# Local attention and an MLP: transposing one head's two parts at a time, and value products on four corners of the array

## The chip, the cores and the metric

The kernel runs on one core of one Trainium2 chip. The time is device microseconds of one execution; the runs shown are compared by their median. Engines are named as in the profile: PE is TensorE's matmul side and PEld its weight loads, DVE is VectorE, ACT is ScalarE, POOL is GpSimd, SP is SyncE, which issues nearly all DMA here.

## What is computed

Local attention for 8 batches and 8 heads over 576 positions of 64 channels, then an MLP over the 4,608 tokens. Every query sees at most 32 keys: heads 0 to 3 the last 32 positions, heads 4 to 7 every fourth of the last 128.

```python
scores = scale * np.matmul(q, k.transpose(0, 1, 3, 2))
scores = np.where(masks[None, :, :, :], scores, -1000000000.0)
scores = scores - np.max(scores, axis=-1, keepdims=True)
attn = np.exp(scores)
attn = attn / (np.sum(attn, axis=-1, keepdims=True) + 1e-09)
out = np.matmul(attn, v)            # [8, 8, 576, 64]
x = out.transpose(0, 2, 1, 3).reshape(4608, 512)
h = x @ w_in                        # w_in 512 x 2048
sp = np.maximum(h, 0.0) + np.log1p(np.exp(-np.abs(h)))
y = (h * erf(sp)) @ w_out           # w_out 2048 x 512
```

## The kernel before, in words

**Units.** A pair of heads of one batch is an item (32 items, heads h = 0 and 1). Its 576 queries are cut in strips of 32; a strip looks at 64 keys. Eight strips are a unit, 72 units in all, and a unit has two parts p = 0, 1 of four strips each.

**One unit's attention.** `scores` (L200): 16 products, a strip and head each, on eight places of PE's array (head h on rows 64h to 64h+63, strip r on columns 32r to 32r+31); head 0's results end in the PSUM bank sp0, head 1's in sp1. The first 256 columns of these banks hold two units' scores in turn. `mask_max` (L211) on DVE adds the mask and takes row maxima, four instructions (part outside, head inside). `exponents` (L221) on ACT, `normalize` on DVE (L232, L233) and POOL (L234). `transposes` (L239): two 128x128 transposes, one per part, each with both heads' 64 keys, into `turn_place`; `turned` (L243) copies the 256 columns to pT in SBUF. `values` (L257): 16 products, strip and head, with 64 keys contracted, 64 channels and 32 queries. Head h's keys lie on partitions 64h and up, its channels on 64h and up, so the products use two corners of the array, (0, 0) and (64, 64). All results of a unit go to `place`: 256 columns of one bank. `rows_hi` (L298) on ACT copies them, rounded, into rows of x, and `rows_lo` (L303) on DVE subtracts to get the rest; both go by the pieces that `pieces` cuts, at item borders and, for the dilated heads, every 144 positions.

**Banks.** The eight PSUM banks are sp0, sp1, tx, h and acc0 to acc3. Units below FREE = 15 use acc banks, (u+1) % 4, for `place` and `turn_place`, since the MLP does not use them yet. Later units use tx for `place` (its second half for the second unit of a pair) and columns 256 to 511 of sp0, or sp1 for the second of a pair, for `turn_place`. The framework that writes the semaphores keeps the order of the program between instructions of two engines on one bank whenever either order could clash, two readers included.

**The order of work** is written out by hand. First 14 first visits (`first_visit`), with visit n doing the scores of unit n and the value products of unit n - 3; weights are read and split meanwhile (`prep_act`, `prep_dve`). Then a loop over half steps x of the MLP: `mm1` (L478) fills bank h, `take` (L486) copies it out on DVE, `mm2` (L519) adds the gated result of two steps before into acc. The table made by `visits` says at which half steps units are attended: one unit each at x = 0 to 6 and at three more, then 25 pairs at 2 to 5 half steps' distance, then the last unit alone. In such a half step `turn` stands ahead of mm2, and `attend` behind it: value products of the ready units, scores of the next ones, row copies; then the maxima.

```python
    def attend(ready, scored):
        for u in ready:
            values(u)
        for u in scored:
            scores(u)
        for u in ready:
            rows_hi(u)
```

## Time and profile before

| | |
|---|---|
| median of 3 runs | 956.28 us (956.1 to 956.96) |
| profiled execution | 957.19 us, span 955.4 us |
| granted clock of the core | 0.998 |
| PE, PEld busy | 931.9 us, 768.3 us |
| ACT, DVE, POOL busy | 633.6, 559.1, 74.3 us |
| HBM read, written | 74.15 MB, 27.26 MB |

A row of a group reads: line, engine, operation, out<-in by the program's names, partitions x elements, count, then busy time, mean of one in ns, and the idle time ahead with what ended it. A row of the order of time reads: start, length, engine, line, the same names, count, and in brackets the idle time ahead. In the table of stretches each engine has its busy time and, in brackets, its number of instructions; behind them the granted clock, the DMA share and GB/s. A product in FP32 stands as two matmul records and two weight loads.

### The profile page before, as it was taken

The page shows a single profiled execution, that of the slowest core. Times are in us where ns is not written, and L with a number is a line of the kernel's source. Part 1 is how long each engine was busy: PE and PEld are TensorE (multiplying, and loading weights), DVE is VectorE, ACT ScalarE, POOL GpSimd, SP SyncE. Part 2 cuts the span into 40 slices and gives each one's busy share as a digit, 9 for nine tenths or more (in the row PEclk, how much of TensorE's full clock was granted, in tenths as well). Part 3 has the DMA queues.
Part 4 walks back from the last instruction along what each step waited for, and adds up shares of the span by engine and source line. Part 5 has one row for each costly group of instructions (what it writes and reads, how often), then busy time and mean ns, then how long its engine had stood idle before and what let it go on. Part 6 is the DMA issues. An engine that isn't in the chain of part 4 may idle for free.

```text
span 955.4 us, 20237 instructions
## 1 busy us (share of the span) xinstructions
PE 931.9 (98%) x8208; PEld 768.3 (80%) x8208; DVE 559.1 (59%) x1569; ACT 633.6 (66%) x1202; POOL 74.3 (8%) x92
## 2 busy tenths in 40 slices
PE   5899999999999999999999999999999999999998
PEld 4677887888888888888888888888888888888886
DVE  6868879886565555555555555655554444434444
ACT  6679878775856866666576674866566556545553
POOL 1211100000000100010000000000000000000000
PEclk9999999999999999999999999999999999999999
DMA  8875544531732242323332271314331202011001
GB/s 283 262 255 171 181 172 137 158 117 57 226 128 71 72 147 84 116 72 116 91 116 71 72 228 48 107 60 139 91 116 38 86 28 89 1 44 45 1 1 44
DMA packets 53821, 103.64 MB, mean 108 GB/s; under 512 B 7136, under 2 KB 20192, under 8 KB 53728
## 3 DMA queue, kind: packets, MB, share of 16 engines
q1 hardware_dynamic: 53440, 101.83, 32.5%
q8 instruction: 64, 1.05, 0.5%
q10 hardware_dynamic: 288, 0.52, 0.1%
q14 instruction: 29, 0.24, 0.1%
HBM read 74.15 MB, written 27.26 MB: 106 GB/s over the span
## 4 chain that ended last, share of the span: by engine, by line
PE 92%; ACT 3%; DVE 2%; DMA 1%; issue 1%; SPq 0%; DVEq 0%
PE h L478 41%; PE acc L519 39%; PE tx L257 6%; PE sp L200 3%; PE acc L257 2%; PE sp L239 1%; DMA dbl<-in_w_in_dram 1%; ACT prob L221 1%; DVE s L501 0%; PE acc L239 0%; DMA qk<-in_qk_dram 0%; DVE w L420 0%; DVE hc L486 0%; DVE w L421 0%; DVE win_lo L415 0%
## 5 line engine op out<-in xcount | busy, mean ns | idle before, releaser
L486 DVE COPY hc<-h 128x512 f32<-128x512 f32 x144 | 99.5, 691 | 290.1 <-PE h L478 289.8
L478 PE MATMUL h<-x,win_hi 128*128 128x512 f32 x832 | 261.2, 395 | 1.5 <-DVE hc L486 1.5
L519 PE MATMUL acc<-wout_hi,ghi 128*128 128x512 f32 x576 | 227.5, 395 | 0.3 <-DVE ghi L504 0.3
L519 PE MATMUL acc<-wout_lo,ghi 128*128 128x512 f32 x576 | 224.7, 390 | 0.0
L490 ACT ACTIVATE s<-hc 128x1024 f32<-128x1024 f32 x72 | 76.5, 1062 | 200.6 <-DVE hc L486 200.2
L478 PEld LDWEIGHTS h<-x,win_hi 128*128 128x128 f32 x832 | 156.4, 190 | 35.1 <-DVE hc L486 1.6
L478 PE MATMUL h<-x,win_lo 128*128 128x512 f32 x416 | 163.5, 393 | 0.0
L519 PE MATMUL acc<-wout_hi,glo 128*128 128x512 f32 x576 | 159.1, 389 | 0.0
L519 PEld LDWEIGHTS acc<-wout_hi,glo 128*128 128x128 f32 x576 | 108.2, 188 | 23.1
L519 PEld LDWEIGHTS acc<-wout_hi,ghi 128*128 128x128 f32 x576 | 108.2, 188 | 22.3 <-DVE ghi L504 0.7
L519 PEld LDWEIGHTS acc<-wout_lo,ghi 128*128 128x128 f32 x576 | 108.2, 188 | 21.7
L234 POOL TENSOR_TENSOR prob<-prob,rinv 128x256 f32<-128x256 f32 x72 | 70.3, 986 | 603.3 <-DVE ssum L232 297.5
L505 DVE TENSOR_TENSOR glo<-s,ghi 128x512 fp32r<-128x512 f32 x144 | 100.0, 695 | 5.1
L221 ACT ACTIVATE prob<-prob,nmax 128x64 f32<-128x64 f32 x288 | 96.3, 337 | 3.0 <-DVE nmax L211 2.6
L501 DVE TENSOR_TENSOR s<-hc,s 128x1024 f32<-128x1024 f32 x72 | 93.5, 1299 | 5.6 <-ACT s L494 5.6
L491 ACT ACT_TABLE_LOAD x72 | 92.4, 1283 | 1.3
L494 ACT ACT_TABLE_LOAD x72 | 92.4, 1283 | 1.3
L478 PEld LDWEIGHTS h<-x,win_lo 128*128 128x128 f32 x416 | 78.8, 190 | 17.1
L211 DVE CUSTOM_DVE_ANT_0 prob<-sp,cst 128x64 f32<-128x64 f32 x288 | 45.4, 220 | 69.0 <-PE sp L200 68.4
L478 PE MATMUL h<-dbl,win_hi 128*128 128x512 f32 x256 | 80.6, 396 | 0.0
L494 ACT ACTIVATE s<-s 128x1024 f32<-128x1024 f32 x72 | 76.4, 1061 | 0.8
L491 ACT ACTIVATE s<-s 128x1024 f32<-128x1024 f32 x72 | 76.3, 1060 | 0.8
(57 smaller groups left out, 911.3 us busy)
## 6 DMA issues: line engine op xcount, KB each, us to landing
v<-in_v_dram SPq DMA_DIRECT2D x72, 256.0 KB, 4.2
xT<-rows SPq DMA_DIRECT2D x26, 576.0 KB, 4.9
qk<-in_qk_dram SPq DMA_DIRECT2D x48, 272.0 KB, 4.2
dbl<-in_w_in_dram SPq DMA_DIRECT2D x16, 512.0 KB, 4.5
dbl<-in_w_out_dram SPq DMA_DIRECT2D x16, 512.0 KB, 3.7
qk<-in_qk_dram SPq DMA_DIRECT2D x24, 288.0 KB, 4.0
out_dram<-w SPq DMA_DIRECT2D x26, 256.0 KB, 2.2
x<-xT SPq DMA_DIRECT2D x8, 320.0 KB, 5.4
```

The source lines that it names most:

```text
L211: nc.vector.tensor_tensor_reduce(out=pr[:, g, :], in0=sps[h][:, u % 2, p, :], in1=mask[QUADS.index(kinds(u, p))], scale=-SCALE, scalar=BIG ...
L221: nc.scalar.activation(out=probs[u][:, j, :], in_=probs[u][:, j, :], func=AF.Exp, scale=-1.0, bias=nmax[:, j:j + 1], accum_out=sums[u][:, ...
L234: nc.gpsimd.tensor_tensor(probs[u], probs[u], rinv.broadcast_to([P, 2 * PARTS, KEYS]), op=ALU.mult)
L257: nc.tensor.matmul(xp[hs, qs], vt[hs, s, :], pt[hs, qs], start=True, stop=True, tile_position=(h * D, h * D))
L478: nc.tensor.matmul(h, w[:, cc, ft * P:(ft + 1) * P], x[cc], start=(k == 0 and i == 0), stop=(k == CC - 1 and i == 2))
L486: nc.vector.tensor_copy(out=hs[t][:, j], in_=h)
L490: nc.scalar.activation(out=ls[t], in_=hs[t], func=AF.Sigmoid, scale=-1.0)
L491: nc.scalar.activation(out=ls[t], in_=ls[t], func=AF.Ln, bias=TINY)
L494: nc.scalar.activation(out=ls[t], in_=ls[t], func=AF.Erf, scale=-1.0)
L501: nc.vector.tensor_tensor(out=e, in0=hc, in1=e, op=ALU.mult)
L505: nc.vector.tensor_tensor(out=glo, in0=e[:, j], in1=ghi.bitcast(F32), op=ALU.subtract)
L519: nc.tensor.matmul(acc[tt], g[:, tt * P:(tt + 1) * P], w[:, ft, :], start=(first and w is wout_hi and g is ghi), stop=(last and g is glo))
```

## The change

The transposes are now one per head, with both parts of that head: keys of part p lie on partitions 64p and up, queries of both heads side by side in the columns. The values v are laid out in DRAM to match. `values` goes over four strips, and for each over part and head: products at all four corners (64p, 64h) of the array. Part 0's and part 1's results go to two banks: acc (u+1) % 4 and (u+3) % 4 for early units, later tx and sp1 (columns 256 to 511, half of them for the second unit of a pair). The maxima run head outside, part inside, and `pieces` cuts every 128 columns as well, so that no piece spans two banks: 208 pieces in place of 144.

```diff
@@ -155,7 +155,7 @@
 
     qkz = [one.tile([P, QW + KW], F32, name=f"qk{i}") for i in range(2)]
 
-    vz = [one.tile([P, SPU, D], F32, name=f"v{i}") for i in range(2)]
+    vz = [one.tile([P, SIDE, 2, D], F32, name=f"v{i}") for i in range(2)]
     pz = [one.tile([P, TOK], F32, name=f"pT{i}") for i in range(2)]
 
     spb = [ps.tile([P, TOK], F32, name=f"sp{i}") for i in range(2)]
@@ -166,13 +166,17 @@
 
     second = set()
 
-    def place(u):
-
-        return acc[(u + 1) % 4] if u < FREE else bank[:, PER * BLK:] if u in second else bank
+    def place(u, p):
+
+
+        if u < FREE:
+            return acc[(u + 1 + 2 * p) % 4][:, p * P:(p + 1) * P]
+        at = p * PARTS * P + (u in second) * P
+        return (spb[1] if p else bank)[:, at:at + P]
 
     def turn_place(u):
 
-        return (place(u) if u < FREE else spb[u in second])[:, PARTS * P:2 * PARTS * P]
+        return (acc[(u + 1) % 4] if u < FREE else spb[u in second])[:, PARTS * P:2 * PARTS * P]
 
 
     xs = [one.tile([P, 2, S], F32R, name=f"x{cc}") for cc in range(CC)]
@@ -185,7 +189,7 @@
 
     def load_v(u):
         if has(u):
-            nc.sync.dma_start(out=vz[u % 2], in_=v[u].rearrange("p (s d) -> p s d", s=SPU))
+            nc.sync.dma_start(out=vz[u % 2], in_=v[u].rearrange("p (s h d) -> p s h d", s=SIDE, h=2))
 
     probs, maxes, sums, x_rows = {}, {}, {}, {}
 
@@ -205,9 +209,9 @@
 
         pr = probs[u] = work.tile([P, 2 * PARTS, KEYS], F32, name="prob", bufs=LAG + 1)
         nmax = maxes[u] = small.tile([P, 2 * PARTS], F32, name="nmax", bufs=LAG + 1)
-        for p in range(PARTS):
-            for h in range(2):
-                g = 2 * p + h
+        for h in range(2):
+            for p in range(PARTS):
+                g = PARTS * h + p
                 nc.vector.tensor_tensor_reduce(
                     out=pr[:, g, :], in0=sps[h][:, u % 2, p, :], in1=mask[QUADS.index(kinds(u, p))],
                     scale=-SCALE, scalar=BIG,
@@ -235,12 +239,12 @@
 
     def transposes(u):
         pr = probs.pop(u)
-        for p in range(PARTS):
-            nc.tensor.transpose(out=turn_place(u)[:, p * P:(p + 1) * P],
-                                in_=pr[:, 2 * p:2 * p + 2, :].rearrange("p h k -> p (h k)"), identity=ident)
+        for h in range(2):
+            nc.tensor.transpose(out=turn_place(u)[:, h * P:(h + 1) * P],
+                                in_=pr[:, PARTS * h:PARTS * (h + 1), :].rearrange("p a k -> p (a k)"), identity=ident)
 
     def turned(u, copy):
-        copy(out=pz[u in second][:, 0:PARTS * P], in_=turn_place(u))
+        copy(out=pz[u in second][:, 0:2 * P], in_=turn_place(u))
 
     def turn(units):
         for u in units:
@@ -249,13 +253,15 @@
             turned(u, nc.vector.tensor_copy)
 
     def values(u):
-        xp, vt, pt = place(u), vz[u % 2], pz[u in second]
-        for s in range(SPU):
+        vt, pt = vz[u % 2], pz[u in second]
+        for s in range(SIDE):
             qs = slice(s * STRIP, (s + 1) * STRIP)
-            for h in range(2):
-                hs = slice(h * D, (h + 1) * D)
-                nc.tensor.matmul(xp[hs, qs], vt[hs, s, :], pt[hs, qs], start=True, stop=True,
-                                 tile_position=(h * D, h * D))
+            for p in range(PARTS):
+                ks, xp = slice(p * KEYS, (p + 1) * KEYS), place(u, p)
+                for h in range(2):
+                    nc.tensor.matmul(xp[h * D:(h + 1) * D, qs], vt[ks, s, h, :],
+                                     pt[ks, h * P + s * STRIP:h * P + (s + 1) * STRIP], start=True, stop=True,
+                                     tile_position=(p * KEYS, h * D))
 
     def attend(ready, scored):
         for u in ready:
@@ -275,7 +281,7 @@
             cuts = sorted({at, at + BLK} | {c for c in range(0, S, RES) if dil and at < c < at + BLK})
             for a, b in zip(cuts, cuts[1:]):
                 res = a // RES if dil else None
-                if got and got[-1][0] == (it, res) and got[-1][2] == a:
+                if got and got[-1][0] == (it, res) and got[-1][2] == a and (src + a - at) % P:
                     got[-1][2] = b
                 else:
                     got.append([(it, res), a, b, src + a - at])
@@ -291,7 +297,7 @@
             else:
                 i = a - res * RES
                 at = slice(i * DIL + res, (i + b - a - 1) * DIL + res + 1, DIL)
-            yield x_rows[it][:, 0, at], x_rows[it][:, 1, at], place(u)[:, c:c + b - a]
+            yield x_rows[it][:, 0, at], x_rows[it][:, 1, at], place(u, c // P)[:, c % P:c % P + b - a]
 
     def rows_hi(u):
         for hi, _, src in rows_of(u):
@@ -697,8 +703,8 @@
 
     p = _padded(a)
     w = np.stack([p[..., i * STRIP:i * STRIP + KEYS, :] for i in range(NSTRIP)], axis=2)
-    w = w.reshape(NU, SPU, 2, KEYS, D).transpose(0, 2, 3, 1, 4)
-    return np.ascontiguousarray(w).reshape(NU, 2 * KEYS, SPU * D)
+    w = w.reshape(NU, PARTS, SIDE, 2, KEYS, D).transpose(0, 1, 4, 2, 3, 5)
+    return np.ascontiguousarray(w).reshape(NU, PARTS * KEYS, SPU * D)
 
 
 def _masks():
```

**Where the order moves.** First PE at the first pair of units, between mm2 and the scores (v1 with pT0 is the first unit, v0 with pT1 the second; tx and sp1 are the banks that are written). Before:

```order
L519 MATMUL acc3_96<-wout_hi_82,glo_2151 128x512
L257 MATMUL tx_92<-pT0_88,v1_87 64x32 [waits DMAHW5_49,DVE_49]
L257 MATMUL tx_92<-pT0_88,v1_87 64x32 x15
L257 MATMUL tx_92<-pT1_89,v0_86 64x32 [waits DMAHW2_49,DVE_49]
L257 MATMUL tx_92<-pT1_89,v0_86 64x32 x15
L200 MATMUL sp0_90<-qk0_84 32x64 [waits DMAHW4_49]
```

Now:

```order
L525 MATMUL acc3_96<-wout_hi_82,glo_2189 128x512
L262 MATMUL tx_92<-pT0_88,v1_87 64x32 [waits DMAHW5_49,DVE_49]
L262 MATMUL tx_92<-pT0_88,v1_87 64x32
L262 MATMUL sp1_91<-pT0_88,v1_87 64x32 [waits DVE_49]
L262 MATMUL sp1_91<-pT0_88,v1_87 64x32
L262 MATMUL tx_92<-pT0_88,v1_87 64x32 x2
L262 MATMUL sp1_91<-pT0_88,v1_87 64x32 x2
...
L262 MATMUL tx_92<-pT1_89,v0_86 64x32 [waits DMAHW2_49]
L262 MATMUL tx_92<-pT1_89,v0_86 64x32
L204 MATMUL sp0_90<-qk0_84 32x64 [waits DMAHW4_49]
```

As many products stand in the same place. Two for tx and two for sp1 alternate, and the wait for DVE's second copy of pT, which reads sp1, has moved from the second unit's first product to the first unit's third.

Then DVE behind the same scores: the maxima of the first of the two units (rows between are left out) and the row subtractions. Before:

```order
L211 ISA prob_2295,nmax_2296<-sp0_90,cst_59 128x64 [waits PE_49]
...
L211 ISA prob_2295,nmax_2296<-sp1_91,cst_59 128x64 [waits PE_49]
...
L303 TENSOR_TENSOR rows_2031<-tx_92,rows_2031 128x256 [waits Activation_49]
L303 TENSOR_TENSOR rows_2031<-tx_92,rows_2031 128x128
L303 TENSOR_TENSOR rows_2289<-tx_92,rows_2289 128x128 [waits DMAHW3_49]
L486 COPY hc_2189<-h_109 128x512 [waits PE_49]
```

Now:

```order
L215 ISA prob_2334,nmax_2335<-sp0_90,cst_59 128x64 [waits PE_49]
...
L215 ISA prob_2334,nmax_2335<-sp1_91,cst_59 128x64 [waits PE_49,Activation_49]
...
L309 TENSOR_TENSOR rows_2067<-tx_92,rows_2067 128x128
L309 TENSOR_TENSOR rows_2067<-sp1_91,rows_2067 128x128
L309 TENSOR_TENSOR rows_2067<-tx_92,rows_2067 128x128
L309 TENSOR_TENSOR rows_2328<-sp1_91,rows_2328 128x128 [waits DMAHW3_49]
L492 COPY hc_2227<-h_109 128x512 [waits PE_49]
```

The maxima from sp1 wait for ACT, whose row copies read that bank just before them in the program; there are four subtractions instead of three ahead of the copy of h.

Last, PE at the fifth unit's value products in the first visits. Before:

```order
L257 MATMUL acc1_94<-pT0_88,v0_86 64x32 [waits DMAHW4_49,Activation_49]
L257 MATMUL acc1_94<-pT0_88,v0_86 64x32 x15
L239 MATMUL acc2_95<-ident_58,prob_390 128x128 [waits Pool_49]
L239 MATMUL acc2_95<-ident_58,prob_390 128x128
L200 MATMUL sp0_90<-qk0_84 32x64 [waits DMAHW6_49,DVE_49]
```

Now:

```order
L262 MATMUL acc1_94<-pT0_88,v0_86 64x32 [waits DMAHW4_49,Activation_49]
L262 MATMUL acc1_94<-pT0_88,v0_86 64x32
L262 MATMUL acc3_96<-pT0_88,v0_86 64x32 x2
...
L243 MATMUL acc2_95<-ident_58,prob_393 128x128 [waits DVE_49,Pool_49]
L243 MATMUL acc2_95<-ident_58,prob_393 128x128
L204 MATMUL sp0_90<-qk0_84 32x64 [waits DMAHW6_49]
```

The next unit's transpose now waits for DVE as well: acc2 holds the second part of the unit before the last, which DVE still subtracts from.

## The prediction, made before the changed kernel had been run

> **What bounds the kernel now.** First the page: the span, the engines, the chain that ended last by engine and by line.
>
> ```profile
> span 955.4 us, 20237 instructions
> PE 931.9 (98%) x8208; PEld 768.3 (80%) x8208; DVE 559.1 (59%) x1569; ACT 633.6 (66%) x1202; POOL 74.3 (8%) x92
> ...
> PE 92%; ACT 3%; DVE 2%; DMA 1%; issue 1%; SPq 0%; DVEq 0%
> PE h L478 41%; PE acc L519 39%; PE tx L257 6%; PE sp L200 3%; PE acc L257 2%; PE sp L239 1%; DMA dbl<-in_w_in_dram 1%; ACT prob L221 1%; DVE s L501 0%; PE acc L239 0%; DMA qk<-in_qk_dram 0%; DVE w L420 0%; DVE hc L486 0%; DVE w L421 0%; DVE win_lo L415 0%
> ```
>
> PE sets the time. L478 and L519 are the MLP and are not touched; the value products of L257 hold 6% + 2% of the chain. Next the table of stretches, which tells where PE time counts (columns: us, then the busy time of each engine):
>
> ```profile
> 20.00:30.00 10.00, 7.67 (x158) 6.40 (x160) 9.76 (x40) 7.80 (x30) 2.50 (x6) 1.00 0.86 255
> 30.00:40.00 10.00, 8.06 (x178) 6.16 (x174) 9.69 (x35) 7.55 (x35) 1.67 (x4) 1.00 0.87 276
> ...
> 90.00:100.00 10.00, 10.00 (x160) 7.90 (x159) 9.70 (x32) 9.43 (x29) 0.38 (x1) 1.00 0.33 109
> ...
> 200.00:400.00 200.00, 200.00 (x1931) 166.03 (x1931) 117.46 (x358) 135.47 (x260) 16.92 (x16) 1.00 0.37 121
> 400.00:800.00 400.00, 400.00 (x3480) 331.60 (x3479) 213.27 (x612) 261.23 (x487) 31.82 (x30) 1.00 0.29 94
> ```
>
> From 200 to 800 us PE is never idle and DVE and ACT have a third to a half to spare: a microsecond less on PE there is one less at the end. From 20 to 40 us DVE is full (19.45 of 20) and PE is not; from 90 to 100 both are.
>
> Then PE in order of time, at one unit alone and at a pair (value products L257, scores L200, next MLP products L478; start and length in us):
>
> ```profile
> 82.99 1.12 PE L257 MATMUL tx<-pT,v 64*64 64x32 f32 x32
> 84.04 0.45 PE L200 MATMUL sp<-qk 64*32 64x64 f32 x32
> 84.42 0.73 PE L478 MATMUL h<-x,win_hi 128*128 128x512 f32 x2
> ...
> 504.12 2.06 PE L257 MATMUL tx<-pT,v 64*64 64x32 f32 x64
> 506.11 0.86 PE L200 MATMUL sp<-qk 64*32 64x64 f32 x64
> 506.89 0.73 PE L478 MATMUL h<-dbl,win_hi 128*128 128x512 f32 x2
> ```
>
> A unit's 16 products stand as 32 records, two each. From the start of one stage to the next, value products take 1.05 us for one unit and 1.99 for two: 0.94 per unit and 0.11 once per visit. They lie on two corners of the array, so each corner works through 16 records at 0.94/16 = 59 ns. The scores are 32 records too, with twice the columns streamed, and take 0.38 us: they lie on eight places (two halves of the rows, four column strips), (0.38 - 0.11)/4 = 68 ns for each of four rounds. So a place takes some 60 ns for a record however many places there are, and records can be issued every 0.27/32 = 8 ns. Two places are the limit of L257.
>
> **The change part by part.** *Four corners.* The same 32 records go to four places, eight rounds: 8 x 59 = 0.47 us, with the 0.11 left as it is 0.58 instead of 1.05: 0.47 less per unit. No row shows this form. What it asks for, two products in one half of the rows with other weights and other streams, and two row halves over the same columns that end in two banks, the scores do already, with four strips in each half. Bounds: 0.38 (the scores' rate) and 1.05 (no overlap gained); order could even cost a little (second rival). I take 0.58, which is nearest to the scores' row in kind.
>
> The row speaks first here; against it stands the Trainium skill, "TensorE: Matmul & The Clock Gate", Part 3, "The mechanism": a weight load overlaps products in flight only where the row group differs. By that rule the two products of one row half would follow each other and the sum would be no gain, 0; the scores, four strips of one half inside 0.38 us, do not agree with it.
>
> *Where it counts.* Units from the schedule in the code: 11 in the first visits, 4 at the first half steps (all on acc: 480 records = 15 units), then 7 alone and 25 pairs (1824 records = 57 units).
>
> ```profile
> L257 PE MATMUL tx<-pT,v 64*64 64x32 f32 x1824 | 59.2, 220 | 1.0 <-DVE pT L243 1.0
> ...
> L257 PE MATMUL acc<-pT,v 64*64 64x32 f32 x480 | 25.6, 273 | 7.4 <-ACT pT L243 5.8 <-DVE pT L243 1.6
> ```
>
> Pairs: 25 x 0.94 = 23.5 us, all from 170 us on, where PE is full. Alone: 7 x 0.47 = 3.3 us, but at one of them PE already waits for DVE's copy of pT:
>
> ```profile
> PEld tx L257 <- DVE pT L243: 1.4, 1, 1.4
> ```
>
> That is the unit at 148 us; what the unit before it saves (0.47) is lost in this wait, and DVE, full at 90 to 100, takes away some 0.4 more. I keep 2.4.
>
> First half steps:
>
> ```profile
> 60.99 1.08 PE acc L257 x32
> 62.09 0.37 ACT rows L298
> 62.48 1.28 ACT L490
> ...
> 72.07 0.33 DVE pT L243
> ```
>
> The chain leaves PE after the second of the four units and runs over ACT and DVE to 75 us. So two units count, 2 x 0.47 = 0.9 us; the other two are covered by that chain.
>
> First visits:
>
> ```profile
> 28.32 0.26 ACT pT L243
> 28.62 1.95 PE acc L257 x32
> 30.75 0.39 ACT x L298
> 31.25 1.10 ACT prob L221 x6
> ...
> 42.82 0.61 PE sp L200 x32
> 43.43 1.85 PE acc L257 x32
> 45.28 0.64 PE acc L239 x2
> ```
>
> A unit lasts 1.85 us there, twice as long as later, so 0.9 us is saved in each. Up to 40 us it goes nowhere: DVE has no room, and gets more work. In the last four visits the chain is on PE alone, 0.61 + 1.85 + 0.64 = 3.1 us a visit; there a new wait takes most: a transpose now writes a bank whose rows DVE still reads, and waits for that subtraction:
>
> ```profile
> 44.10 0.72 DVE L303 TENSOR_TENSOR x<-acc,x 128x80 fp32r<-128x80 f32 x3
> ```
>
> It ends at 44.8, and the old transpose starts at 45.3. I count 0.3 x 4 = 1.2 gained and 0.7 lost earlier (0.16 in each of some four visits): 0.5.
>
> *More row copies.* Pieces are now cut at 128 columns: 208 instead of 144 on ACT and again on DVE, 64 more each. DVE, start to start:
>
> ```profile
> 28.46 0.42 DVE L303 TENSOR_TENSOR x<-acc,x 128x256 fp32r<-128x256 f32 x1
> 28.80 1.13 DVE L415 TENSOR_TENSOR win_lo<-w,win_hi 128x512 fp32r<-128x512 f32 x1
> ...
> 32.44 0.59 DVE L303 TENSOR_TENSOR x<-acc,x 128x128 fp32r<-128x128 f32 x2
> 32.94 1.03 DVE L415 TENSOR_TENSOR win_lo<-w,win_hi 128x512 fp32r<-128x512 f32 x1
> ```
>
> One piece of 256 takes 0.34, two of 128 take 0.50: 0.16 each, 10 us over all. From 170 us on they lie under PE; in the first visits and at 90 to 148 us they are in the losses above. Without PE as cover they would cost the 10 us.
>
> *Transposes, loads.* As many, as large, the same queue order: 0.
>
> *New waits in a pair.* The first product into the second bank waits for DVE's second pT copy, the maxima from that bank wait until ACT has copied the rows out of it. The pair at 504 us:
>
> ```profile
> 501.62 0.75 DVE L243 COPY pT<-sp 128x256 f32<-128x256 f32 x2
> ...
> 506.22 1.02 ACT L298 CAST rows<-tx 128x128 fp32r<-128x128 f32 x5 [6.49 <-PE tx L257]
> 506.98 0.23 DVE L211 CUSTOM_DVE_ANT_0 prob<-sp,cst 128x64 f32<-128x64 f32 x1 [3.55 <-PE sp L200]
> 508.14 1.23 DVE L303 TENSOR_TENSOR rows<-tx,rows 128x128 fp32r<-128x128 f32 x5
> 509.95 0.69 DVE L486 COPY hc<-h 128x512 f32<-128x512 f32 x1 [0.57 <-PE h L478]
> ...
> 512.24 0.41 PEld L478 LDWEIGHTS h<-dbl,win_hi 128*128 128x128 f32 x2
> ```
>
> The pT copies end at 502.4, the value products start at 504.12. With these 0.94 shorter, scores end at 506.0. ACT may read the second bank only then and needs some five pieces of 0.2: 507.1. DVE's six later maxima (0.15 each) end at 508.0, seven subtractions of 0.25 at 509.7. The copy of h, which PE has ready at 509.0, is thus 0.7 late and ends at 510.4; the next L478 comes at 511.3. It stays covered, by 0.9 of the 1.6 us there are now. PE's own new wait costs nothing while the copies are ready, and perhaps something for the semaphore: the second unit of scores in a pair, which begins with one, takes 0.78 - 0.38 = 0.40 against 0.27, while the second unit of value products, which begins with one too, takes the plain 0.94. Bounds 0 and 0.13 a pair; I take 0.04 x 25 = 1.0, nearer to the value products.
>
> **Sum:** 23.5 + 2.4 + 0.9 + 0.5 - 1.0 = 26.3 us less. The profiled execution took 957.19 us, 1.8 around its span of 955.4; the median of the runs is 0.9 lower. 957.2 - 26.3 = 930.9 for a profiled one, 930.0 for the median. Own range, by the bounds of the fixed cost, the early stages and the waits: 926 to 935.
>
> **The rivals.**
> 1. *Half the overlap.* The weight loads of one row half share a path: scores load 4 x 32 columns in 68 ns, 1.9 a ns; the new form wants 2 x 64 in 59, 2.2. At 1.9 a round takes 68 ns, 0.07 more a unit, 934. If 64-column loads get only half of the way, the gain is 12 to 13 us: 943. For it: no row with such loads. Against it: the scores are that close already.
> 2. *No overlap in a row half.* Products come in the order upper, upper, lower, lower half. If two of one half exclude each other, the second upper holds up the first lower behind it; only neighbours of different halves run together, and four products last two turns of 118 ns plus two issue steps of 8, 0.25 us instead of 0.235: 0.06 more a unit, 61 units, 3.8 us, and with the 2 us of row copies on a full DVE and the 1.0 of waits 963: slower. It decides as soon as the round of four exceeds 235 ns. The skill's rule above points here; the scores' 0.38 speaks against it.
> 3. *DVE becomes late.* The wait for ACT's rows delays the copy of h by more than the 1.6 us. Each microsecond beyond costs one per pair; where it is 1, the whole gain of the pairs goes: 954. For it: ACT at 66% can be busy when the rows come. Against it: the 0.9 left over above.
> 4. *PE is relieved but follows DVE up to 200 us:* only the pairs' gain stays, 934; inside the range.
>
> **How the numbers follow.** The forecast with its near neighbours (4, and 1 at 934) 0.80; rival 1 at 943 0.08; rival 2 0.07; rival 3 0.05. The time is 930.0. For eight in ten the range goes from 925 to 942, as the half overlap lies just outside. A measurement of this kernel tells 0.2%, 1.9 us, from no change. Faster: 0.80 + 0.08 and 0.02 of rival 3, 0.90; the other 0.03 of rival 3 is no change; slower is rival 2, 0.07.
>
> **What would show it.** Right: a lone unit's value products last 0.58 us to the scores and a pair's 1.05; their share of the chain falls from 6% to some 3%; PE stays at 97% or more of a span near 929; L478 waits for no copy of h after 170 us; DVE's maxima wait for ACT in the pairs. Wrong: a pair still at 1.9 or more (rival 2) or at 1.5 (rival 1); idle time of PE before L478 in each visit (rival 3); first visits longer than 4.2 us, so that the early loss is larger than I took it.

## The result and the profile after

The changed kernel takes 927.25 us (median of 4 runs, 926.43 to 927.60), the kernel before, beside it on the same chip, 956.62 us (956.10 to 957.03). The ratio is 0.9692, 95% interval 0.9675 to 0.9709: 29.4 us less. Forecast were 26.3 us less, 930.0 us, in a range from 925 to 942. The profiled execution of the change took 926.43 us with a span of 924.6, that of before 957.19 with 955.4: 30.8 us apart, and the accounts by place below are made against these 30.8.

Lines of the program have moved: value products are now L262 (before L257), scores L204 (L200), transposes L243 (L239), the copies of pT L247 (L243), maxima L215 (L211), exponentials L225 (L221), POOL's multiplication L238 (L234), row copies L304 on ACT (L298) and L309 on DVE (L303), the MLP's products L484 and L525 (L478, L519), the copy of h L492 (L486), the split of win_lo L421 (L415).

Of the page of the change, the engines and the chain that ended last:

```profile
PE 895.2 (97%) x8208; PEld 730.8 (79%) x8208; DVE 561.4 (61%) x1633; ACT 638.2 (69%) x1266; POOL 75.4 (8%) x92
...
PE 90%; DVE 5%; ACT 2%; DMA 2%; issue 1%; SPq 0%; POOL 0%; DVEq 0%; ACTq 0%
PE h L484 42%; PE acc L525 40%; PE tx L262 3%; PE sp L204 3%; PE sp L243 1%; DMA dbl<-in_w_in_dram 1%; DVE w L426 1%; DVE w L427 1%; DMA qk<-in_qk_dram 1%; PE sp L262 1%; DVE win_lo L421 1%; DVE prob L215 0%; DVE w L425 0%; DVE s L507 0%; D
```

PE has 36.7 us less of busy time (931.9 to 895.2) with as many records, and is still 97% of the span. Of the chain that ended last, the value products of the late units hold 3% (tx) and 1% (sp) now, where they held 6%; those of the early units (acc) held 2% and hold under 1%. DVE has 5% of the chain instead of 2%; that is new and lies in the first visits, below.

The table of stretches (us, then the busy time of PE, PEld, DVE, ACT, POOL):

```profile
20.00:30.00 10.00, 6.17 (x174) 4.11 (x173) 9.79 (x46) 8.53 (x39) 1.93 (x5) 1.00 0.92 315
...
200.00:400.00 200.00, 200.00 (x1970) 164.65 (x1969) 121.27 (x381) 144.08 (x305) 18.97 (x18) 1.00 0.36 120
400.00:800.00 400.00, 400.00 (x3423) 329.42 (x3422) 218.13 (x620) 264.43 (x483) 29.82 (x28) 1.00 0.28 90
```

From 200 to 800 us PE is still never idle, so that each microsecond taken from it there has come off the end. The granted clock of the late stretches is 1.00, as before. The 1.00 of the early one is no measurement: this trace has no record of the clock ahead of 51.43 us (see the last section).

One unit alone and a pair, in order of time (start, length; the value products' records now alternate between the two banks tx and sp, so that a unit stands in many short rows, of which the first stands here, with the first row of the next stage):

```profile
85.27 0.14 PEld L262 LDWEIGHTS tx<-pT,v 64*64 64x64 f32 x2 [0.35 <-issue]
...
85.87 0.29 PEld L204 LDWEIGHTS sp<-qk 64*32 64x32 f32 x32
...
502.94 0.14 PEld L262 LDWEIGHTS tx<-pT,v 64*64 64x64 f32 x2 [0.35 <-DVE s L507]
...
504.00 0.70 PEld L204 LDWEIGHTS sp<-qk 64*32 64x32 f32 x64
...
504.79 0.30 PEld L484 LDWEIGHTS h<-dbl,win_hi 128*128 128x128 f32 x2
```

Alone, a unit takes 0.60 us to the scores (before 1.05), a pair 1.06 (before 1.99). A pair is 0.60 + 0.47: the second unit costs its eight rounds and nothing more. Behind it stand DVE's and ACT's steps of the same pair:

```profile
504.88 0.23 DVE L215 CUSTOM_DVE_ANT_0 prob<-sp,cst 128x64 f32<-128x64 f32 x1 [0.74 <-PE sp L204]
504.93 0.39 ACT L304 CAST rows<-sp 128x64 fp32r<-128x64 f32 x2 [0.41 <-PE sp L204]
...
505.81 0.23 DVE L215 CUSTOM_DVE_ANT_0 prob<-sp,cst 128x64 f32<-128x64 f32 x1 [0.55 <-ACT rows L304]
...
506.69 0.44 DVE L309 TENSOR_TENSOR rows<-tx,rows 128x48 fp32r<-128x48 f32 x2
...
508.06 0.69 DVE L492 COPY hc<-h 128x512 f32<-128x512 f32 x1
```

The new waits are both there: ACT's rows wait for the scores, since their bank is the scores' own, and DVE's maxima wait 0.55 us for ACT's rows. The waits from 90 us to the end, summed (us in total, times, longest):

```profile
DVE hc L492 <- PE h L484: 270.7, 116, 3.7
...
ACT rows L304 <- PE sp L204: 11.4, 24, 0.6
DVE prob L215 <- ACT rows L304: 9.9, 23, 0.6
...
PEld tx L262 <- DVE pT L247: 1.2, 1, 1.2
```

24 and 23 times, about once a pair, each at most 0.6. DVE waits for PE's h 116 times, and in this list PE waits for no copy of h: the new waits stop at DVE.

Where the 30.8 us come from, by the starts of the value products in both traces (V0 is the start of those of the first unit, V1 of the second, and so on):

| stretch | before | after | less |
|---|---|---|---|
| up to the first unit (V0) | 12.65 | 11.96 | 0.7 |
| first visits, V0 to V11 | 12.65 to 56.35 | 11.96 to 52.80 | 2.9 |
| first half steps, V11 to V15 | 56.35 to 82.98 | 52.80 to 78.37 | 1.1 |
| six units alone, to the first pair | 82.98 to 172.07 | 78.37 to 164.95 | 2.5 |
| 25 pairs, to the last unit | 172.07 to 753.87 | 164.95 to 723.62 | 23.1 |
| last unit, to the end of the span | 753.87 to 955.4 | 723.62 to 924.6 | 0.5 |

V0's start varies from 11.7 to 12.9 over all kernels below with no order in it, so the first row is chance. The row of the first visits is one execution of each kernel too: in three more traces with the change's early code (runs 8, 10 and 11) V0 to V11 takes 41.2, 40.0 and 40.7 us against 40.8 here, and in two more with the old early code (runs 6 and 7) 43.7 and 44.1 against 43.7.

### The profile page after: what moved, and what is told of

Same layout as the page of the kernel before. It is cut to its first block, busy times and chain, and to the rows that moved or that the text cites. A ratio compares the mean times of both kernels' runs of the same rounds, so it can differ in the third digit from the quotient of the medians.

```text
span 924.6 us, 20394 instructions
## 1 busy us (share of the span) xinstructions
PE 895.2 (97%) x8208; PEld 730.8 (79%) x8208; DVE 561.4 (61%) x1633; ACT 638.2 (69%) x1266; POOL 75.4 (8%) x92
## 3 DMA queue, kind: packets, MB, share of 16 engines
q8 instruction: 64, 1.05, 0.5%
## 4 chain that ended last, share of the span: by engine, by line
PE 90%; DVE 5%; ACT 2%; DMA 2%; issue 1%; SPq 0%; POOL 0%; DVEq 0%; ACTq 0%
PE h L484 42%; PE acc L525 40%; PE tx L262 3%; PE sp L204 3%; PE sp L243 1%; DMA dbl<-in_w_in_dram 1%; DVE w L426 1%; DVE w L427 1%; DMA qk<-in_qk_dram 1%; PE sp L262 1%; DVE win_lo L421 1%; DVE prob L215 0%; DVE w L425 0%; DVE s L507 0%; DVE x L309 0%
## 5 line engine op out<-in xcount | busy, mean ns | idle before, releaser
L492 DVE COPY hc<-h 128x512 f32<-128x512 f32 x144 | 99.4, 691 | 273.1 <-PE h L484 273.0
L484 PE MATMUL h<-x,win_hi 128*128 128x512 f32 x832 | 260.7, 395 | 2.1 <-DVE hc L492 1.9
L525 PE MATMUL acc<-wout_hi,ghi 128*128 128x512 f32 x576 | 227.6, 395 | 0.4 <-DVE ghi L510 0.2
L525 PE MATMUL acc<-wout_lo,ghi 128*128 128x512 f32 x576 | 224.6, 390 | 0.0
L484 PEld LDWEIGHTS h<-x,win_hi 128*128 128x128 f32 x832 | 156.1, 189 | 35.7 <-DVE hc L492 2.5
L484 PE MATMUL h<-x,win_lo 128*128 128x512 f32 x416 | 163.5, 393 | 0.0
L525 PE MATMUL acc<-wout_hi,glo 128*128 128x512 f32 x576 | 159.0, 389 | 0.0
L525 PEld LDWEIGHTS acc<-wout_hi,glo 128*128 128x128 f32 x576 | 108.1, 188 | 23.0
L525 PEld LDWEIGHTS acc<-wout_hi,ghi 128*128 128x128 f32 x576 | 108.2, 188 | 22.8 <-DVE ghi L510 0.6
L525 PEld LDWEIGHTS acc<-wout_lo,ghi 128*128 128x128 f32 x576 | 108.2, 188 | 21.6
L238 POOL TENSOR_TENSOR prob<-prob,rinv 128x256 f32<-128x256 f32 x72 | 70.9, 995 | 578.6 <-DVE ssum L236 282.6
L225 ACT ACTIVATE prob<-prob,nmax 128x64 f32<-128x64 f32 x288 | 96.4, 338 | 3.1 <-DVE nmax L215 2.7
L484 PEld LDWEIGHTS h<-x,win_lo 128*128 128x128 f32 x416 | 78.8, 189 | 17.0
L215 DVE CUSTOM_DVE_ANT_0 prob<-sp,cst 128x64 f32<-128x64 f32 x288 | 47.1, 220 | 56.9 <-PE sp L204 47.0
L484 PE MATMUL h<-dbl,win_hi 128*128 128x512 f32 x256 | 80.6, 396 | 0.0
```

Of the source, the lines that this page charges most:

```text
L215: nc.vector.tensor_tensor_reduce(out=pr[:, g, :], in0=sps[h][:, u % 2, p, :], in1=mask[QUADS.index(kinds(u, p))], scale=-SCALE, scalar=BIG ...
L225: nc.scalar.activation(out=probs[u][:, j, :], in_=probs[u][:, j, :], func=AF.Exp, scale=-1.0, bias=nmax[:, j:j + 1], accum_out=sums[u][:, ...
L238: nc.gpsimd.tensor_tensor(probs[u], probs[u], rinv.broadcast_to([P, 2 * PARTS, KEYS]), op=ALU.mult)
L484: nc.tensor.matmul(h, w[:, cc, ft * P:(ft + 1) * P], x[cc], start=(k == 0 and i == 0), stop=(k == CC - 1 and i == 2))
L492: nc.vector.tensor_copy(out=hs[t][:, j], in_=h)
L525: nc.tensor.matmul(acc[tt], g[:, tt * P:(tt + 1) * P], w[:, ft, :], start=(first and w is wout_hi and g is ghi), stop=(last and g is glo))
```

## The experiments

The edits are shortened to the lines that matter. Their ratios are against the kernel before, run beside them on the same chip.

**1. The order of a unit's products.** By the second rival, two products in one half of the rows exclude each other, and only the order (upper, upper, lower, lower) lets halves run side by side. So the same products were put in an order in which all eight of part 0 (upper half) come before those of part 1:

```
-        for s in range(SIDE):
-            for p in range(PARTS):
+        for p in range(PARTS):
+            for s in range(SIDE):
                 for h in range(2):
```

> The changed kernel with the value products of a unit ordered by part: first all eight of part 0 (upper row half, the two column places), then all eight of part 1. Theory (a place takes 59 ns a record, and two places of one row half run side by side): only two places work at a time, 16 records each, so a lone unit takes 0.94 + 0.11 = 1.05 us again and a pair 1.99; the 57 late units and two of the early ones lose 0.47 us each, 0.9 us in some early ones, time 954 to 957. Rival (two products of one row half exclude each other): 32 records in turn, 1.88 + 0.11 = 2.0 us a unit, time near 1012.

Measured: 936.63 us, ratio 0.9794 [0.9778, 0.9810]. Neither came true. A unit alone takes 0.852 us, a pair 1.385. The pair in its trace:

```profile
509.80 0.48 PE L262 MATMUL tx<-pT,v 64*64 64x32 f32 x10
510.07 0.25 PE L262 MATMUL sp<-pT,v 64*64 64x32 f32 x2
...
511.19 0.86 PE L204 MATMUL sp<-qk 64*32 64x64 f32 x64
```

tx holds part 0, in the upper half, and sp part 1, in the lower. Ten records of part 0 start alone, and 0.27 us after the first the lower half starts and both go on. Had the halves followed each other, a unit would have kept its 1.05; had two products of one half excluded each other, part 0's eight products alone would have taken 8 x 0.117 = 0.94. So the exclusion is out, and my own picture (two places work, then two others) was too crude as well.

**2. By head**, so that both row halves are in use but only one half of the columns at a time:

```
+        for h in range(2):
             for s in range(SIDE):
                 for p in range(PARTS):
-                    for h in range(2):
```

> The changed kernel with the value products of a unit ordered by head: first the eight of head 0 (left columns, both row halves, two banks), then the eight of head 1. Theory (two row halves over the same columns run side by side when they end in two banks): 1.05 us a lone unit, time 954 to 957, as by part. Rival (two row halves over the same columns exclude each other): 2.0 us a unit, time near 1012.

Measured: 937.76 us, 0.9808 [0.9786, 0.9830], alone 0.852, pair 1.386: the same loss as by part. Halves of the rows and halves of the columns are alike; what counts is how many products for one place come in a row.

**3. Upper and lower half in turn** (strip, head, part), every product next to one of the other half:

> The changed kernel with the four corners issued in another order: upper left, lower left, upper right, lower right, so that neighbours in the order lie in different row halves. Theory (each corner is busy on its own and the order of issue does not matter): 0.60 us a lone unit, 1.07 a pair, time 927 within 0.2%. Rival (part of the overlap is lost where neighbours in the order share a row half): shorter value products than 0.60, time below 925.

Measured: 926.44 us, 0.9688 [0.9671, 0.9704], alone 0.598, pair 1.065. No difference from the change.

From the first two came a theory: products are taken in strictly in the program's order, and a place holds one that runs and one that waits behind it; a third for the same place stops all behind it. The Trainium skill, "TensorE: Matmul & The Clock Gate", Part 3, "The mechanism", says more than that: matrix products start and end in the program's order. The trace of run 1 does not agree for the starts. At the lone unit at 86.32 us the last records of part 0 start 0.31 to 0.44 us after its first, and part 1, which stands behind them in the program, has started at 0.27. So it is the taking in that keeps the order; a product that has been taken in waits for its place, and one for a free place may start ahead of it. Two runs test the theory at both ends.

**4. Blocks of two strips:** four products for the upper places, four for the lower, and again, so that every place gets two in a row.

```
-        for s in range(SIDE):
-            for p in range(PARTS):
+        for b, p, i in [(b, p, i) for b in range(0, SIDE, 2) for p in range(PARTS) for i in range(2)]:
+            for s in [b + i]:
```

> The changed kernel with the products of a unit in blocks: part 0 of strips 0 and 1 (four products on the two upper places), part 1 of strips 0 and 1 (four on the two lower places), then strips 2 and 3 in the same way. Theory now (products are issued strictly in order, and a place holds one product that runs, 0.117 us, and one that waits behind it): the four of a block all find room, so the other row half starts at once. Lone unit 0.60 us, pair 1.065, 926.5 to 927.6 us. Rival (a row half that has got its products holds up the other until half of them are done, which also gives the 0.25 us of the order by part): the lower places start 0.12 later, lone unit 0.72, pair 1.19: 25 x 0.12 = 3 and 0.8 in the early part, 931 us.

Measured: 926.84 us, 0.9682 [0.9668, 0.9697]; alone 0.618, pair 1.085, 0.02 above the change. The theory held.

**5. One place after the other:** all four products of a corner, then the next corner (part, head, strip).

> The changed kernel with a unit's 16 products ordered by place: four on one corner, then four on the next. Theory (in order; one runs and one waits at each place): the third product of a corner is taken in after 0.117 us, the fourth after 0.234, only then the next corner's first. Corners start at 0, 0.23, 0.47 and 0.70: lone unit 0.70 + 0.47 + 0.13 = 1.30 us instead of 0.60, and in a pair the second unit starts at 0.94: pair 2.24 instead of 1.065. 25 x 1.17 = 29.3, and 0.7/0.25 of the 1.6 us that the order by part cost outside of the pairs, 4.5: 961 us, 957 to 966. Rival 1 (one place at a time when neighbours in the order are on the same place): 16 x 0.117 = 1.87, lone 1.98, pair 3.85: 1006 us. Rival 2 (a place takes in all its four products; the loss in the order by part has another cause): no corner waits, lone 0.60, 927 us.

Measured: 973.10 us, 1.0168 [1.0151, 1.0185]; alone 1.36 us, pair 2.40. The pair:

```profile
514.50 0.73 PE L262 MATMUL tx<-pT,v 64*64 64x32 f32 x13
515.02 0.24 PE L262 MATMUL sp<-pT,v 64*64 64x32 f32 x1
...
516.90 0.86 PE L204 MATMUL sp<-qk 64*32 64x64 f32 x64
```

The first record of the third corner (part 1, in sp) starts 0.52 us after the first corner's: 0.26 for each corner, against the 0.23 of the theory, and 3 x 0.26 + 0.43 for the last corner's records + 0.15 is the 1.36. The records of a lone unit (at 94.23 us) show what the corner waits for: its third product starts at 0.254 us (0.079 to the second record, then three steps of 0.058), and the next corner's first record stands 0.006 behind. So the fourth product finds room when the third starts, as the theory has it. Both rivals (1.98 or 0.60 alone) are out. The time was mis-sized: 961 expected, 973.1 measured. The pairs explain 25 x (2.40 - 1.065) = 33.4 of the 45.9 us above the change; in the first visits and half steps the loss is 8.4 us by the starts of the units, and the units alone, 7 x 0.76, bring at most 5.3. I had scaled the early part from the 1.6 us that I took the order by part to have lost outside of the pairs (by the medians 936.63 - 927.25 - 25 x 0.32 = 1.4), where most was covered.

So the same 16 products on the same four corners make this kernel 3.1% faster or 1.7% slower, by their order alone.

**6. Only the more finely cut row copies**, put into the kernel before:

```
-                if got and got[-1][0] == (it, res) and got[-1][2] == a:
+                if got and got[-1][0] == (it, res) and got[-1][2] == a and (src + a - at) % P:
```

> The kernel before with one line of the change: row pieces are cut every 128 columns too, 208 instead of 144 on ACT and on DVE. Theory (PE covers them from 170 us on, DVE is full earlier): 0.16 us each for some 18 units that count, 0 to 3 us more, 956.6 to 959.6. Rivals: nothing at all (956.6), or all 64 on the path (0.16 x 64 = 10 us, 967).

Measured: 956.75 us over 10 runs, 1.0006 [0.9996, 1.0015]. The 64 added pieces on each engine cost nothing, in the first visits either.

**7 and 8. The change in the late units alone** (from unit 15 on) **and in the first 15 alone**; the others keep the old form, with the old layout of keys and rows:

```
+    def new(u):
+        return u >= FREE      # and u < FREE in the other
```

> The change for units 15 to 71 alone; the first 15 units (first visits and first half steps) are transposed and multiplied as before, with uncut pieces. Theory (the gains of the two stages add up, and the traces put 4.6 us of the gain ahead of the first unit on tx): 932. Rival (the early gain is a chance of the DMA's start, or is given back when DVE is late at 148 us): 927 to 929.

Measured: 931.43 us, 0.9734 [0.9719, 0.9748].

> The change for units 0 to 14 alone, all later ones as before. Theory: 956.6 - 4.6 = 952. My prediction's own sum: 0.5 + 0.9 less, 955.2. Rival: as before, 956.6.

Measured: 952.61 us, 0.9957 [0.9945, 0.9969], with more scatter than any other kernel here (949.8 to 954.8 over 10). The early units bring 4.0 us alone and 931.43 - 927.25 = 4.2 on top of the others; the parts add up (25.2 + 4.0 = 29.2 of 29.4). The prediction gave the early units 1.4.

**9. The transposes' wait for DVE taken away:** part 1 of the early units goes to other banks, so that a transpose no longer writes a bank whose rows DVE still reads.

```
-            return acc[(u + 1 + 2 * p) % 4][:, p * P:(p + 1) * P]
+            b = (h if u % 2 and u < FIRST - LAG else bank) if p else acc[(u + 1) % 4]
+            return b[:, p * P:(p + 1) * P]
```

> The changed kernel with part 1's results of units 0 to 14 put into banks that nothing else uses then (tx, and h for odd units of the first visits) in place of acc (u+3) % 4, so that a transpose no longer waits for DVE's row subtraction. Theory (this wait ends last at some visits: the trace shows 1.3 us of PE idle put down to it in three of them, the others wait for POOL, ACT or DMA): 0 to 1.5 us less, 926 to 927. Rival (the prediction's account: it takes most of the gain in the last four visits, 0.5 us each and more): 2 to 3 us less, 924 to 925.

Measured: 926.61 us, 0.9683 [0.9668, 0.9697], not to be told from the change. So the time does not show the wait, but the trace does. From one unit's value products to the next's (us; the early code of runs 8, 10 and 11 is that of the change):

| | V7 to V8 | V8 to V9 | V9 to V10 | V10 to V11 |
|---|---|---|---|---|
| before | 3.07 | 3.09 | 3.07 | 6.83 |
| change | 2.63 | 4.48 | 2.64 | 5.99 |
| runs 8, 10, 11 | 2.63 to 2.67 | 2.87 | 2.81, 2.82 | 6.40, 5.89, 6.37 |
| run 9, without the wait | 2.24 | 4.05 | 2.24 | 6.84 |

A visit with the wait takes 2.63 to 2.87 us, one without it 2.24. The 4.48 and the 4.05 are loads of q and k that land late in these two executions (at 43.3 and 44.0 us, 6.2 and 5.4 us after their start; the same load takes 4.0 to 4.5 us in runs 8, 10 and 11). What run 9 gains there is gone by V11, in part because nine of the twelve MLP products on the way run at half the clock, against six in the change (last section). With the wait, the chain goes through it, here in run 10:

```profile
41.16 0.71 DVE x L309 x4
...
42.01 0.66 PE acc L243 x2
42.66 0.72 PE sp L204 x32
```

So the wait does set the pace of these visits where no load is late, and run 9's time says only that taking it away does not shorten the whole.

**10 and 11. What if the row copies were more?** The rows of the pairs' units cut at every 64 and at every 32 columns: 236 and 424 pieces instead of 147 on ACT and again on DVE.

```
-                ... and got[-1][2] == a and (src + a - at) % P:
+                ... and got[-1][2] == a and (src + a - at) % (P if u < 22 else 64):
```

The second has 32 in place of 64, and a cut in the middle of each block of 64 besides.

> The changed kernel with the rows of the pairs' units cut at every 64 columns: 236 pieces instead of 147 over the 25 pairs, 3.6 more in a pair, on ACT and again on DVE behind it. At 0.16 a piece on each engine the copy of h comes 1.1 us later in a pair. Theory (the copy is 0.26 late at the pair at 503 us, so 1.3 of the 1.6 us are left as cover): covered, 926.5 to 928 us. Rival (the prediction's own numbers: 0.7 late, 0.9 left): 0.2 comes through in each pair, 932 us.

Measured: 926.70 us, 0.9685 [0.9670, 0.9699].

> The same with a cut every 32 columns: 424 pieces instead of 147, 11.1 more in a pair, 1.8 us on ACT and 1.8 on DVE, the copy of h 3.6 later. Theory (1.3 left as cover): 2.2 comes through in each pair, 25 x 2.2 = 55, 982 us. With the prediction's 0.9 left: 2.7, 993 us. Rival (ACT's and DVE's copies lie beside each other and not behind each other, since DVE has maxima to do while ACT copies): 1.8 later, 0.5 comes through, 939 us.

Measured: 927.53 us, 0.9688 [0.9674, 0.9703]. Both are within the scatter of the change, and all three expectations for the second were far off. Its DVE at a pair whose value products start at 504.40:

```profile
508.56 0.62 DVE L309 TENSOR_TENSOR rows<-tx,rows 128x32 fp32r<-128x32 f32 x5
...
510.54 0.69 DVE L492 COPY hc<-h 128x512 f32<-128x512 f32 x1
```

and its PE at the same place:

```profile
509.13 0.39 PE L525 MATMUL acc<-wout_hi,ghi 128*128 128x512 f32 x1
...
511.85 0.61 PE L484 MATMUL h<-dbl,win_hi 128*128 128x512 f32 x2
```

18 subtractions take 1.98 us start to start, where the change's 8 take 508.06 - 506.69 = 1.37: 0.06 a piece, not the 0.16 I had used. Over the pairs, DVE's busy time from 160 us on grows from 428.5 to 444.9 for 277 pieces, 0.06 again. The copy of h is 1.25 us late here (PE had h when L525 started at 509.13, its last product ended about 0.16 later) and ends about 0.6 before PE comes back for the next L484: nothing comes through. The edge of the cover was not reached, and is not known closer than that.

**12. DVE's room in the first visits.** In the kernel before, the split of win_lo took 0.99 to 1.14 us in six first visits (the row at 28.80 in the prediction) and 0.68 or 0.69 in the 26 other cases of this line (10 of win_lo, 16 of wout_lo); in each of the six, POOL's multiplication starts 0.02 to 0.16 us ahead of it (in the one below, 0.03):

```profile
28.77 0.61 POOL L234 TENSOR_TENSOR prob<-prob,rinv 128x256 f32<-128x256 f32 x1
```

One edit to the kernel before moves POOL's addition to the sums, so that this multiplication starts earlier:

```
 def exponents(u):
-        if u < FIRST:
-            nc.gpsimd.tensor_scalar(sums[u], sums[u], 1.0e-9, None, op0=ALU.add)
 def normalize(u):
+        if u < FIRST:
+            nc.gpsimd.tensor_scalar(sums[u], sums[u], 1.0e-9, None, op0=ALU.add)
```

> The kernel before with one edit: in the first visits the small addition to a unit's sums on POOL is issued two visits later, ahead of that unit's reciprocal, so that POOL's multiplication no longer stands in its queue behind an addition that waits for ACT. In the kernel before the multiplication (0.61 us) starts within 0.03 us of the split of win_lo on DVE in six visits, and the split takes 0.99 to 1.14 us there against 0.68 in the 26 other cases. Theory (the two exclude each other; DVE was full from 20 to 40 us through this only): POOL starts 0.9 earlier, beside the maxima, the six splits take 0.68, DVE has 2.4 us less to do, and the time falls by about 2, to 954.3 to 955.5. Rival (the length of the split has another cause, or DVE's time in the first visits is not what counts): splits still at 1.0 to 1.1, or the time within 0.5 of the kernel before.

Measured: 956.12 us against 957.06, 0.9991 [0.9982, 1.0000]. Half of the theory is right:

```profile
27.55 0.61 POOL L234 TENSOR_TENSOR prob<-prob,rinv 128x256 f32<-128x256 f32 x1 [2.82 <-DVE rinv L233]
...
28.82 0.68 DVE L415 TENSOR_TENSOR win_lo<-w,win_hi 128x512 fp32r<-128x512 f32 x1
```

POOL is 1.2 us earlier, the split takes 0.68 in all six visits, and DVE has 8.84 us of work from 20 to 30 us instead of 9.76. And up to V6 it is worth nothing: the seventh unit's value products start at 36.81 us, before at 36.80. DVE's fullness was not what set the pace of these visits. V7 does come 0.3 us sooner (39.99 against 40.29), since the chain of before passes DVE there, and from V10 to V11 the run is 0.7 us shorter, with five of the MLP's twelve products at half the clock instead of eight (last section). The 0.94 us less in the median are at the edge of the interval, and less than half of the theory's 2.

That both parts write one bank wasn't tried. What the second bank is worth in itself stays open.

## Why the prediction was right, and where it was wrong

**What bounds the kernel, and the pairs: right.** "Two places are the limit of L257" and "eight rounds" give 23.5 us; measured 23.1. A unit alone was to take 0.58 and takes 0.60. In a place the records start 58 ns apart (59 forecast), and the four places' records 6.5 ns apart. No overlap in a row half (rival 2) and half the overlap (rival 1) are refuted by the 0.60 and by the order by part: two products of one half, with other weights, run side by side from the start. With that falls, for this form, the rule of the Trainium skill that the prediction weighed ("TensorE: Matmul & The Clock Gate", Part 3, "The mechanism"): as the prediction works it out, it gives a unit 1.05 us, and the trace has 0.60.

But the prediction took the places alone for the limit and did not work out what the order of a unit's products does; here it does no harm. Rival 2 asked the right question (who is held up by a product that can't start) with the wrong blocker: a product is held up when a third for one place stands ahead of it, not by its neighbour in the half. The change's order never has more than one in a row for a place.

**Units alone: right, a little low.** 2.4 forecast, 3.0 measured (2.5 and 0.5 in the table). The stall at the unit at 148 us is still there (1.2 us, before 1.4), as the prediction had it.

**First half steps: right.** 0.9 forecast, 1.1 measured. Two units lie on the chain and two don't:

```profile
52.87 0.60 PE acc L262 x32
...
56.98 0.61 PE acc L262 x32
...
57.61 0.43 ACT rows L304 x2
```

**First visits: wrong up to V7, right behind it.** The step that failed is "Up to 40 us it goes nowhere: DVE has no room, and gets more work", and with it "0.7 lost earlier". Measured from V0 to V7: 27.64 us before, 25.09 after, 2.5 gained where 0.7 was to be lost (1.2 to 1.9 gained in runs 8, 10 and 11). DVE at 97% is a share and no chain. The chain of the kernel before, with a visit's pieces in order:

```profile
20.61 1.95 PE acc L257 x32
...
22.69 0.33 ACT x L298
23.01 0.19 ACT prob L221
...
23.24 1.09 ACT prob L221 x6
24.33 0.27 ACT pT L243
...
24.64 1.94 PE acc L257 x32
```

It is a ring of PE and ACT: value products 1.95, then on ACT a row copy 0.33, exponentials 1.28 and the copy of pT 0.27, and the next unit's value products: 4.03 from 20.61 to 24.64, with DVE nowhere in it. So it goes up to V5 at 32.66; from 35.9 to 40.2 us, ahead of V7, the chain of before does run over DVE. Rows of the same kind from a later visit stood in the prediction itself, which read a length of L257 in them and not a ring. DVE's time was as full as that in part because its split of win_lo stood up to 0.46 us longer beside POOL in six visits; run 12 took that out (9.76 to 8.84 of 10 us) and the ring went on at 4.0. Shorter value products (1.85 to 1.01 at the early rate, which is that of half the clock, last section) shorten the ring to some 3.2, and then DVE does bound the visit:

```profile
26.19 0.40 DVE x L309 x2
26.59 0.60 DVE win_lo L421
27.19 0.35 DVE w L425
27.56 0.70 DVE w L426
28.29 0.69 DVE w L427
28.98 0.09 DVE rinv L237
...
29.62 0.50 DVE x L309 x2
```

That is the change's chain from 12 to 37 us, DVE and nothing else, 3.4 us a visit where nothing holds it up (26.19 to 29.62) and 3.6 on average. So of 0.84 us a unit some 0.36 a visit arrived here. In run 10 the chain leaves DVE for ACT at 28.7 us, and in runs 8 and 11 it waits for loads until 23 and 18 us. What the prediction said of DVE is true after the change, not before it.

For the last four visits it forecast 0.3 each, the rest lost to the transposes' new wait. That is what runs 8, 10 and 11 show: V7 to V10 takes 8.32 to 8.36 us against 9.24 before, 0.3 a visit, with the new wait on the chain (run 9). In the trace of the change itself these visits lost 0.5 (9.76), by one load that the scores of a visit had to wait for until 43.38:

```profile
37.16 6.19 DMA qk<-in_qk_dram
```

That the change brings such late loads about is not shown; run 9 has one too. V10 to V11 gained 0.8 in this trace, and some 0.3 to 0.4 of it is two products fewer at half the clock. Together: 0.5 forecast, 2.9 measured (2.5 to 3.7 in runs 8, 10 and 11), and 0.7 by chance ahead of V0.

**More row copies: right in the sum, wrong in the price.** They cost nothing (run 6). A piece costs 0.06 us in the pairs, not 0.16, so the "10 us" without cover would have been about 4. The 0.16 came from two rows, and in one of them the second piece of 128 columns took 0.30 us. The other pieces of 128 take 0.20 and those of 256 take 0.34 start to start, in the first visits and later, so a cut costs 0.06 there too.

**New waits in a pair: the waits are right, the price is wrong.** DVE waits for ACT, 23 times, as forecast. The copy of h was to be 0.7 late; at the pair shown it starts at 508.06 where PE had h at about 507.8, 0.26 late, since the row copies on DVE are shorter. The 0.04 x 25 = 1.0 for PE's semaphore is nothing: a pair is 0.598 + 0.467, and 0.467 is eight rounds. Rival 3 (DVE becomes late) is refuted with room to spare, as 1.25 us of lateness in run 11 comes to nothing. Rival 4 (the gain is only the pairs') is out too: the units alone, the first half steps and the first visits bring 7.0.

**Sum.** 23.1 + 3.0 + 1.1 + 2.9 + 0.7 = 30.8 of the profiled executions' 30.8, against 23.5 + 2.4 + 0.9 + 0.5 - 1.0 = 26.3. The miss of 2.7 us in the median (927.25 against 930.0) is of the size of what was missed in the first visits (2.4) and the waits (1.0).

## What to carry to other kernels

Small products go faster when all four corners of the array work, and then by the number of records at one place; order them so that no place gets more than two in a row before the others have theirs (two in a row cost 0.02 us a unit, four 0.25 to 0.76; three weren't run). A full engine in a table of stretches bounds nothing until it stands in the chain, and its busy time may be a wait for another engine: read the ring of pieces in one visit, add up its period, and ask who is next when one piece shrinks. Price a copy from many of its kind, not from the first two rows that show it. And compare a stage of some microseconds over several traces: one late load hid here that a part of the forecast had come true.

## What the runs showed of the hardware

- A place takes in one product behind the running one; a third for it stops all that stand behind it in the program. This is worked out from runs 1, 2, 4 and 5: with two in a row nothing stops (0.618 us a unit), with four in a row the next place starts 0.26 us late, when the third of the four has started, alike for halves of the rows and of the columns (0.852 us in both).
- In a place, fp32 records of 64 x 64 weights and 32 columns start 58 ns apart behind the first visits and 107 ns apart in them (a unit of the change 0.60 and 1.01 us), in both kernels. By the traces the reason is PE's clock. The MLP's products ahead of V11 change their pace in the same way in the kernel before, and the trace's records of the clock begin at that point, 55.39 us:

```profile
54.42 1.05 PE L478 MATMUL h<-x,win_hi 128*128 128x512 f32 x2
55.27 0.46 PE L478 MATMUL h<-x,win_lo 128*128 128x512 f32 x1
55.57 0.63 PE L478 MATMUL h<-x,win_hi 128*128 128x512 f32 x2
56.04 0.39 PE L478 MATMUL h<-x,win_lo 128*128 128x512 f32 x1
```

Two products take 0.85 us from 54.42 and 0.47 from 55.57. From 75.87 to 79.29 us the same trace has a record of half the clock, and two products take 0.85 there as well (77.83 to 78.68). In each of the 14 traces a product takes 0.43 us up to its first record of the clock, which is of 1.00, at 50.4 to 58.7 us. A table that prints 1.00 ahead of it, as those of the prediction and the one above do between 20 and 40 us, has no record there. When the clock goes up moves from run to run: 5 to 11 of the twelve products ahead of V11 are slow. The later stretch at half the clock is missing in the traces of runs 3, 4, 8 and 9, which take 9.4 to 9.7 us from V14 to V15 where the change takes 10.5; so differences of a microsecond between early stages of two traces can be the clock's.
- POOL's multiplication and DVE's subtraction of two operands in SBUF exclude each other: 0.68 us becomes 0.99 to 1.14 when POOL starts 0.02 to 0.16 us ahead of it, and 0.68 again when POOL is moved. In all six cases the subtraction ends 0.54 or 0.55 us after POOL's multiplication has ended. In the change one multiplication started after DVE and took 1.11 instead of 0.61 itself:

```profile
30.08 1.11 POOL L238 TENSOR_TENSOR prob<-prob,rinv 128x256 f32<-128x256 f32 x1
```

The Trainium skill, "SBUF — State Buffer", "SBUF: two separate sides", has this as an exclusive lock between the two engines, which the first to start holds for its whole instruction; these rows agree with it in both directions.
